# Loading and splitting the second third of queries and keys pair by pair in an attention kernel

## The chip, the cores and the metric

The kernel runs on one core of a Trainium2 chip. The metric is the device time of one execution in microseconds, as the median of three timed runs. The engines are TensorE (PE in the profile, with its weight load as PEld), VectorE (DVE), ScalarE (ACT), GpSimd (POOL) and SyncE (SP), which issues most transfers.

## The reference

```python
def _attn_ref(q, k, v):                       # 8 batches, 12 heads, 448 positions, 64 per head
    scores = scale * np.matmul(q, k.transpose(0, 1, 3, 2))
    scores = np.where(mask, -1000000000.0, scores)       # causal
    scores = scores - np.max(scores, axis=-1, keepdims=True)
    attn = np.exp(scores)
    attn = attn / (np.sum(attn, axis=-1, keepdims=True) + 1e-09)
    return np.matmul(attn, v).astype(np.float32)

def reference(**kwargs):
    attn_out = _attn_ref(**attn_kwargs)
    x = attn_out.transpose(0, 2, 1, 3).reshape(B * S, H * D)      # 3584 x 768
    return _moe_ref(x=x, **moe_kwargs)        # top-1 of 8 experts, 80 rows each, relu MLP 768-1024-768
```

All inputs are float32. The mixture of experts picks for each of 3584 rows the expert with the largest logit, keeps the 80 rows of an expert with the largest gate weights, and writes zero elsewhere.

## The kernel before

Attention comes first. Two heads form a pair, and 48 pairs (8 batches of 6) are worked one after the other. Queries and keys come from memory in *thirds*: a third is two pairs (a third of a batch's six), so third 0 holds pairs 0 and 1, third 1 holds pairs 2 and 3, third 2 holds pairs 4 and 5. `load_third` issues its transfers on SyncE: one for the queries and four for the keys, since the keys of each head are stored twice, once for each half of the partitions (`kf[0]`, `kf[1]`). Third 0 alone is loaded pair by pair. The buffers are two, so that third 2 takes the place of third 0.

Scores are wanted nearly in float32 but multiplied in float16. So each number is split: a high half (a cast to float16) and a low half (the number less its high half). `split_third` makes them: `q_high` and `k_high` cast, `q_low` and `k_low` subtract. For thirds 1 to 3 the casts are on DVE (half of third 1's queries on ACT), from third 4 on the query casts are POOL's; the subtractions are POOL's, except some of third 0, which are DVE's. A tile of scores is one product with the high half of the keys and one with the low half (L423 and L424 in the profile; the last rows of both heads share a tile, L433 to L436).

Each pair is worked in eight slots. Slots 0 to 6 give seven tiles of scores, slot 7 the product of probabilities and values of two pairs before (`xp`, L495). Behind a tile DVE masks it and takes the row minimum (L445, into `ns` and `nb`), and ACT takes the exponential into `prob` (L448). In slots 0, 2, 4 and 6 TensorE transposes the pair before's probabilities (L465), which ACT or DVE copies out (L477). The tiles of scores go round three banks, so a tile's products wait until the masking of the tile three before it is done. DVE copies a finished pair out (`xu`, L500).

The order on each engine is the order in which the program is written. What is not part of the eight slots is put in by a table: `later_on(slot, ...)` puts an operation at the end of a slot, counted from the start (pair n begins at slot 8n), and `third_plan` places the parts of a split by lists of such slots, `SECOND` for third 1 (counted from slot 0), `THIRD_EARLY` for thirds 2 and 3, counted from one slot after the third before begins. `late_constants` puts small constants of the routing at slots 19, 27, 35 and 43, on POOL: `identb` and `before`, `wgd`, `slots_e` with `slots_t` and `mv`, and the last memsets.

Each engine works through its own order and stops at an instruction whose inputs or buffers are not ready. After the last pair the mixture of experts follows, with weights loaded in pieces, products with weights split in the same way, and indirect transfers of the rows.

Of the kernel before, what the change touches and what calls it, by code (L numbers as in the profile page):

```python
# [35 lines left out]
THIRD = [0, 0, 2, 2, 4, 6, 8]  # L36
THIRD_NEXT = [0, 0, 6, 2, 6, 4, 8]
THIRD_EARLY = [0, 2, 4, 6, 4, 6, 8, 10]
SECOND = [8, 10, 6, 6, 10, 8, 12, 14]
ORDER_FIRST = [(0, 0), (1, 0), (2, 0), (0, 1), (1, 1), (2, 1)]  # L40
LATE = 19

# [10 lines left out]
def attention_then_moe(  # L53
# [12 lines left out]
    nc = tc.nc  # L66
# [71 lines left out]
    HB = 3  # L138
    PH = NP // HB
# [169 lines left out]
    lo, hi = slice(0, DH), slice(DH, P)  # L309

    def load_third(h):

        b, hf = h // HB, h % HB
        at = [0]

        def t32(n):
            at[0] += 1
            return qk_bufs[h % 2][:, (at[0] - 1) * PH * S:at[0] * PH * S].rearrange("k (p s) -> k p s", s=S)
        st = state[h] = {}
        st["qf"], st["kf"] = qf, kf = t32("qf"), [t32("kfa"), t32("kfb")]  # L320
        p0 = hf * PH
        for x in [slice(i, i + 1) for i in range(PH)] if h == 0 else [slice(0, PH)]:
            ps = slice(p0 + x.start, p0 + x.stop)

            begin = h == 0 and x.start == 0
            nc.sync.dma_start(qf[:, x], qT[b, :, ps, :])
            for j, rows in enumerate((lo, hi)):
                (nc.scalar if begin else nc.sync).dma_start(kf[j][lo, x], kT[b, rows, ps, :])
                nc.sync.dma_start(kf[j][hi, x], kT[b, rows, ps, :])
# [10 lines left out]
    def split_third(h):  # L340
# [3 lines left out]
        qf, kf = st["qf"], st["kf"]  # L344
        for x, nm in enumerate(("qa", "qb", "ka", "kb", "la", "lb")):
            st[nm] = qk_parts[h % 2][:, x * PH * S:(x + 1) * PH * S].rearrange("k (p s) -> k p s", s=S)
        qa, qb, k_hi, k_lo = st["qa"], st["qb"], (st["ka"], st["kb"]), (st["la"], st["lb"])

        sub = lambda e, o, a, b: e.tensor_tensor(out=o, in0=a, in1=b, op=ALU.subtract)  # L349
        v, g = nc.vector, nc.gpsimd  # L350
# [28 lines left out]
        def by_turns(x):  # L379
            def q_high(js=(0, 1)):  # L380

                for j in js:
                    copy = nc.gpsimd.tensor_copy if h > HB else nc.scalar.copy if h == 1 and j else nc.vector.tensor_copy
                    copy((qa, qb)[j][(lo, hi)[j], x], qf[(lo, hi)[j], x])  # L384

            def k_high(j):
                nc.vector.tensor_copy(k_hi[j][:, x], kf[j][:, x])  # L387

            def q_low(i):
                nc.gpsimd.tensor_tensor(out=qa[hi, i], in0=qf[lo, i], in1=qa[lo, i], op=ALU.subtract)  # L390
                nc.gpsimd.tensor_tensor(out=qb[lo, i], in0=qf[hi, i], in1=qb[hi, i], op=ALU.subtract)  # L391

            def k_low(i):
                for j in range(2):
                    nc.gpsimd.tensor_tensor(out=k_lo[j][:, i], in0=kf[j][:, i], in1=k_hi[j][:, i], op=ALU.subtract)  # L395
            lows = [f for i in range(x.start, x.stop) for f in (lambda i=i: q_low(i), lambda i=i: k_low(i))]
            highs = [q_high, lambda: k_high(0), lambda: k_high(1)]
            if h < HB + 1:
                return highs[1:] + [lambda: q_high([0]), lambda: q_high([1])] + [lows[1], lows[0]] + [f for i in range(1, PH) for f in (lows[2 * i + 1], lows[2 * i])]
            return highs + lows  # L400
# [575 lines left out]
        assert not steps  # L976

    def third_plan(h, slot):
        for x, f in zip(SECOND if h == 1 else THIRD_EARLY if h < HB + 1 else THIRD_NEXT if h % HB == 1 else THIRD, split_third(h)):
            later_on(slot + x, [f])  # L980

    with tc.manual_schedule():
# [26 lines left out]
        for i, pr in enumerate(pairs):  # L1009
# [8 lines left out]
            h = i // PH  # L1018
# [404 lines left out]
```

## Time and profile before

| | us |
|---|---|
| median of three timed runs | 470.98 |
| lowest and highest of them | 470.6 and 471.75 |
| the profiled execution | 472.62 |
| its span, first to last instruction | 470.9 |
| busy in the span: PE | 439.9 (93%) |
| DVE | 416.8 (89%) |
| ACT | 397.5 (84%) |
| POOL | 315.2 (67%) |
| mean granted TensorE clock | 0.985 of full |

Busy time is a mean over stages with different limits: POOL's 67% is made of a first half near 9 tenths and a tail with little work. The profiled execution's time is longer than its span by 1.72 us, which lie around the instructions.

### The profile page before, as it was taken

To read this page: it belongs to the slowest core of one execution; us is meant where nothing else is said; L and a number is where in the kernel's file an instruction comes from. 1 tells how busy PE (TensorE), PEld (TensorE's weight loads), DVE (VectorE), ACT (ScalarE), POOL (GpSimd) and SP (SyncE) were. 2 spreads that over 40 slices of the span, in tenths; PEclk is the share of its full clock that TensorE was granted. 3 is DMA by queue.
4 is the path that set the end of the run, shared out by engine and by line. 5 is a ranking of instruction groups with operands and counts; after the bars stand their busy time and mean duration, and the time that the engine had idled before them with its cause. 6 is when DMAs were issued, how large, how long until landed. Compare 5 with 4: busy or idle time off the path is not lost.

```text
span 470.9 us, 14816 instructions
## 1 busy us (share of the span) xinstructions
PE 439.9 (93%) x5279; PEld 344.2 (73%) x5279; DVE 416.8 (89%) x1279; ACT 397.5 (84%) x1076; POOL 315.2 (67%) x382
## 2 busy tenths in 40 slices
PE   4799999999999999999999999999989899898994
PEld 2566667866777777777777677676559899898994
DVE  5788889988998999899899989988589999998892
ACT  6798989878988897898889889887596999987992
POOL 7899999988987997897899699740361265400101
PEclk9799999999999999999999999999999999998998
DMA  7858899989769579776956967549939999999911
GB/s 215 185 151 235 266 291 246 274 251 314 197 200 295 170 217 290 219 222 203 289 178 209 308 172 229 171 168 378 386 112 333 410 388 390 387 423 427 386 38 43
DMA packets 43001, 120.88 MB, mean 257 GB/s; under 512 B 6146, under 2 KB 23810, under 8 KB 39472
## 3 DMA queue, kind: packets, MB, share of 16 engines
q1 hardware_dynamic: 41712, 116.21, 76.1%
q0 software_dynamic: 1056, 3.51, 2.4%
q8 instruction: 41, 0.67, 0.6%
q10 hardware_dynamic: 160, 0.23, 0.2%
q14 instruction: 32, 0.26, 0.2%
HBM read 96.36 MB, written 23.99 MB: 256 GB/s over the span
## 4 chain that ended last, share of the span: by engine, by line
PE 83%; DVE 7%; DMA 4%; issue 3%; SPq 1%; ACT 1%; POOLq 0%; DVEq 0%; POOL 0%; ACTq 0%
PE xp L495 17%; PE tp L465 16%; PE sp L423 7%; PE sp L424 5%; PE rt L592 4%; PE hp L1231 3%; DMA qk<-k_t 3%; PE sp L433 3%; PE gp L545 3%; PE hp L1241 3%; PE hp L1238 3%; PE hp L1240 3%; PE op L1241 3%; PE op L1238 3%; PE op L1240 3%
## 5 line engine op out<-in xcount | busy, mean ns | idle before, releaser
L448 ACT ACTIVATE prob<-ns,nb 128x128 f32<-128x128 f32 (+3 forms) x336 | 176.9, 528 | 23.7 <-DVE nb L445 21.7
L445 DVE CUSTOM_DVE_ANT_0 ns<-sp,mask 128x384 f32<-128x384 f32 (+2 forms) x288 | 116.1, 414 | 18.7 <-PE sp L424 14.8
L465 PE MATMUL tp<-ident,prob 128*128 128x128 f32 x768 | 118.0, 276 | 0.9 <-ACT prob L448 0.9
L477 ACT COPY PT<-tp 128x512 f32<-128x512 f32 x182 | 103.9, 572 | 17.6 <-PE sp L423 8.4
L395 POOL TENSOR_TENSOR qk<-qk,qk 128x448 f16<-128x448 f32 x92 | 96.4, 1069 | 14.2 <-DVE qk L387 8.6
L1165 DVE SCALAR_TENSOR_TENSOR wl<-wraw,wh 128x768 f16<-128x768 f32 (+1 forms) x98 | 98.1, 1062 | 4.0 <-ACT yt L1304 1.1
L465 PEld LDWEIGHTS tp<-ident,prob 128*128 128x128 f32 x768 | 89.7, 142 | 11.2 <-ACT PT L477 1.6
L495 PE MATMUL xp<-PT,vt 128*64 128x448 f32 (+3 forms) x768 | 91.1, 380 | 0.0
L1180 ACT ACTIVATE wh<-wraw 128x768 f16<-128x768 f32 (+1 forms) x98 | 84.7, 926 | 6.8 <-PE hp L1241 3.3
L495 PEld LDWEIGHTS xp<-PT,vt 128*64 128x64 f32 x768 | 53.8, 137 | 42.7 <-issue 22.7
L423 PE MATMUL sp<-qk 128*128 128x384 f16 (+2 forms) x288 | 75.7, 278 | 9.2 <-ACT qk L355 5.1
L424 PE MATMUL sp<-qk 128*128 128x384 f16 (+2 forms) x288 | 78.1, 277 | 1.2 <-DVE qk L349 0.4
L1241 PEld LDWEIGHTS <-wl 128*128 128x128 f16 x668 | 67.5, 101 | 3.2 <-issue 2.8
L1238 PEld LDWEIGHTS <-wh 128*128 128x128 f16 x668 | 67.9, 102 | 1.6 <-issue 1.6
L1240 PEld LDWEIGHTS <-wh 128*128 128x128 f16 x668 | 67.5, 101 | 1.1 <-issue 1.0
L1319 POOL DMA_INDIRECT out<-yo,idx x8 | 21.9, 2743 | 68.0 <-ACT yo L1316 64.8
L448 ACT ACTIVATION_READ_ACCUMULATOR prob<-ns,nb 128x1 f32 x336 | 63.7, 189 | 0.0
L390 POOL TENSOR_TENSOR qk<-qk,qk 64x448 f16<-64x448 f32 x46 | 53.7, 1168 | 4.0 <-DVE qk L384 0.6
L391 POOL TENSOR_TENSOR qk<-qk,qk 64x448 f16<-64x448 f32 x46 | 51.2, 1114 | 3.2
L387 DVE CAST qk<-qk 128x896 f16<-128x896 f32 x46 | 40.8, 888 | 0.9 <-DMA qk<-k_t 0.9
L384 POOL CAST qk<-qk 64x896 f16<-64x896 f32 x40 | 37.9, 948 | 4.3 <-PE sp L436 3.1
L423 PEld LDWEIGHTS <-qk 128*128 128x128 f16 x288 | 28.5, 99 | 16.8 <-issue 7.8
(188 smaller groups left out, 905.1 us busy)
## 6 DMA issues: line engine op xcount, KB each, us to landing
wraw<-w SPq DMA_DIRECT2D x27, 1536.0 KB, 22.0
qk<-k_t SPq DMA_DIRECT2D x92, 224.0 KB, 6.0
out<-mask_l SPq DMA_DIRECT2D x56, 192.0 KB, 4.5
qk<-q_t SPq DMA_DIRECT2D x23, 448.0 KB, 4.8
vt<-v_t SPq DMA_DIRECT2D x24, 384.0 KB, 5.9
xs<-xr SPq DMA_DIRECT2D x42, 192.0 KB, 3.8
wraw<-w SPq DMA_DIRECT2D x24, 256.0 KB, 4.8
vt<-v_t SPq DMA_DIRECT2D x24, 64.0 KB, 5.3
```

Source lines behind the costliest of these rows:

```text
L395: nc.gpsimd.tensor_tensor(out=k_lo[j][:, i], in0=kf[j][:, i], in1=k_hi[j][:, i], op=ALU.subtract)
L423: nc.tensor.matmul(sp[:, 0:w], qx[:, p, t * P:w], kx[:, p, 0:w], start=True, stop=False)
L424: nc.tensor.matmul(sp[:, 0:w], qx[:, p, t * P:w], lx[:, p, 0:w], start=False, stop=True)
L445: pr.masked = nc.vector.tensor_tensor_reduce(out=ns[:, 0:w], in0=sp[:, 0:w], in1=m, scale=-1.0 / 8.0, scalar=HUGE, op0=ALU.add, op1=ALU.mi ...
L448: nc.scalar.activation(pr.P[:, off:off + w], ns[:, 0:w], AF.Exp, bias=nb, scale=-1.0, accum_out=total)
L465: nc.tensor.transpose(pr.tp[:, i], pr.P[:, off:off + P], ident)
L477: copy(dst, src)
L495: state["pe"] = nc.tensor.matmul(xp[rows, 0:w], st["vt"][:, c, p * P + j * DH:p * P + (j + 1) * DH], pr.PT[:, j, n0:n0 + w], start=(c == 0 ...
L1165: return nc.vector.scalar_tensor_tensor(out=l, in0=src, scalar=SW, in1=h, op0=ALU.mult, op1=ALU.subtract)
L1238: nc.tensor.matmul(o, wh[:, ws], ah[:, c, :], start=(x == 0 and i % per == 0), stop=False, skip_group_check=True)
L1240: nc.tensor.matmul(o, wh[:, ws], al[:, c, :], start=False, stop=False, skip_group_check=True)
L1241: nc.tensor.matmul(o, wl[:, ws], ah[:, c, :], start=False, stop=(x == n - 1), skip_group_check=True)
```

## The change

Third 1 is loaded pair by pair, as third 0 was: ten transfers of half the size instead of five. Its split is made pair by pair too, in eleven steps at slots 8 to 15 instead of eight steps at slots 6 to 14: for its first pair (pair 2) the casts of queries (one half on DVE, one on ACT), two casts of keys on DVE, the query subtractions on POOL, and the two key subtractions on DVE instead of POOL; for its second pair (pair 3) the same, with all subtractions on POOL. Third 2, which was split in slots 17 to 27, is now split in slots 24 to 29 by a list of its own. All later thirds keep their slots.

```diff
--- before.py
+++ after.py
@@ -36,7 +36,8 @@
 THIRD = [0, 0, 2, 2, 4, 6, 8]
 THIRD_NEXT = [0, 0, 6, 2, 6, 4, 8]
 THIRD_EARLY = [0, 2, 4, 6, 4, 6, 8, 10]
-SECOND = [8, 10, 6, 6, 10, 8, 12, 14]
+SECOND = [8, 10, 11, 9, 11, 12, 13, 14, 15, 14, 15]
+THIRD_2 = [7, 8, 9, 10, 9, 10, 11, 12]
 ORDER_FIRST = [(0, 0), (1, 0), (2, 0), (0, 1), (1, 1), (2, 1)]
 LATE = 19
 
@@ -319,7 +320,7 @@
         st = state[h] = {}
         st["qf"], st["kf"] = qf, kf = t32("qf"), [t32("kfa"), t32("kfb")]
         p0 = hf * PH
-        for x in [slice(i, i + 1) for i in range(PH)] if h == 0 else [slice(0, PH)]:
+        for x in [slice(i, i + 1) for i in range(PH)] if h < 2 else [slice(0, PH)]:
             ps = slice(p0 + x.start, p0 + x.stop)
 
             begin = h == 0 and x.start == 0
@@ -393,6 +394,19 @@
             def k_low(i):
                 for j in range(2):
                     nc.gpsimd.tensor_tensor(out=k_lo[j][:, i], in0=kf[j][:, i], in1=k_hi[j][:, i], op=ALU.subtract)
+            def q_first(x):
+                v.tensor_copy(qa[lo, x], qf[lo, x])
+                nc.scalar.copy(qb[hi, x], qf[hi, x])
+
+            def k_first(j, x):
+                v.tensor_copy(k_hi[j][:, x], kf[j][:, x])
+
+            if h == 1:
+                a, b = slice(0, 1), slice(1, 2)
+                return [lambda: q_first(a), lambda: k_first(0, a), lambda: k_first(1, a), lambda: q_low(0),
+                        lambda: sub(v, k_lo[0][:, a], kf[0][:, a], k_hi[0][:, a]),
+                        lambda: sub(v, k_lo[1][:, a], kf[1][:, a], k_hi[1][:, a]),
+                        lambda: q_first(b), lambda: k_first(0, b), lambda: k_first(1, b), lambda: q_low(1), lambda: k_low(1)]
             lows = [f for i in range(x.start, x.stop) for f in (lambda i=i: q_low(i), lambda i=i: k_low(i))]
             highs = [q_high, lambda: k_high(0), lambda: k_high(1)]
             if h < HB + 1:
@@ -976,7 +990,7 @@
         assert not steps
 
     def third_plan(h, slot):
-        for x, f in zip(SECOND if h == 1 else THIRD_EARLY if h < HB + 1 else THIRD_NEXT if h % HB == 1 else THIRD, split_third(h)):
+        for x, f in zip(SECOND if h == 1 else THIRD_2 if h == 2 else THIRD_EARLY if h < HB + 1 else THIRD_NEXT if h % HB == 1 else THIRD, split_third(h)):
             later_on(slot + x, [f])
 
     with tc.manual_schedule():
```

What this does to the order of two engines. In the rows below `qk_112` and `qk_113` are the loaded queries and keys of even and odd thirds, `qk_0_114` and `qk_1_115` their halves, `ns,nb<-sp` a masking.

VectorE from the end of pair 0 through pair 1, before (casts of third 1 into `qk_1_115`):

```order
L384 CAST qk_1_115<-qk_113 64x896
L445 ISA ns,nb<-sp,mask_l 128x448
L445 ISA nb 128x1
L445 ISA ns,nb<-sp,mask 128x128
L445 ISA nb 128x1
L387 CAST qk_1_115<-qk_113 128x896
L445 ISA ns,nb<-sp,mask 128x128
L445 ISA nb 128x1
L445 ISA ns,nb<-sp,mask 128x256
L445 ISA nb 128x1
L387 CAST qk_1_115<-qk_113 128x896
L445 ISA ns,nb<-sp,mask 128x256
```

and after:

```order
L459 ISA ns,nb<-sp,mask 128x128
L459 ISA nb 128x1
L398 CAST qk_1_115<-qk_113 64x448
L459 ISA ns,nb<-sp,mask 128x128
L459 ISA nb 128x1
L459 ISA ns,nb<-sp,mask 128x256
L459 ISA nb 128x1
L402 CAST qk_1_115<-qk_113 128x448
L459 ISA ns,nb<-sp,mask 128x256
L459 ISA nb 128x1
L402 CAST qk_1_115<-qk_113 128x448
L350 TENSOR_TENSOR qk_1_115<-qk_113,qk_1_115 128x448
```

The whole-third cast ahead of pair 0's last masking and the whole-third key casts behind it are gone; casts of one pair stand two maskings later, and a subtraction follows them.

VectorE in the maskings before which third 2 (`qk_0_114`) is cast; before, in pair 2:

```order
L445 ISA ns,nb<-sp,mask 128x128
L445 ISA nb 128x1
L445 ISA ns,nb<-sp,mask 128x128
L445 ISA nb 128x1
L387 CAST qk_0_114<-qk_112 128x896
L445 ISA ns,nb<-sp,mask 128x256
L445 ISA nb 128x1
L445 ISA ns,nb<-sp,mask 128x256
L445 ISA nb 128x1
L387 CAST qk_0_114<-qk_112 128x896
L445 ISA ns,nb<-sp,mask 128x384
```

and after, in pair 3:

```order
L459 ISA ns,nb<-sp,mask 128x128
L459 ISA nb 128x1
L514 COPY xu<-xp 128x448
L388 CAST qk_0_114<-qk_112 128x896
L459 ISA ns,nb<-sp,mask 128x128
L459 ISA nb 128x1
L388 CAST qk_0_114<-qk_112 128x896
L459 ISA ns,nb<-sp,mask 128x256
L459 ISA nb 128x1
L385 CAST qk_0_114<-qk_112 64x896
L459 ISA ns,nb<-sp,mask 128x256
```

The four casts of third 2 have moved from pair 2 to pair 3, where they stand behind the copy of pair 0's output and have one masking, not two, between them.

GpSimd from the first constants on, before:

```order
L262 CAST identb<-ident 128x128
L265 MEMSET before 128x512
L267 AFFINE_SELECT before<-before 128x128
L395 TENSOR_TENSOR qk_0_114<-qk_112,qk_0_114 128x448 x2
L390 TENSOR_TENSOR qk_0_114<-qk_112,qk_0_114 64x448
L391 TENSOR_TENSOR qk_0_114<-qk_112,qk_0_114 64x448
L395 TENSOR_TENSOR qk_0_114<-qk_112,qk_0_114 128x448 x2
L273 MEMSET wgd 128x192
L276 COPY wgd<-lg 64x3x8 x4
L390 TENSOR_TENSOR qk_0_114<-qk_112,qk_0_114 64x448
L391 TENSOR_TENSOR qk_0_114<-qk_112,qk_0_114 64x448
```

and after:

```order
L263 CAST identb<-ident 128x128
L266 MEMSET before 128x512
L268 AFFINE_SELECT before<-before 128x128
L396 TENSOR_TENSOR qk_0_114<-qk_112,qk_0_114 128x448 x2
L274 MEMSET wgd 128x192
L277 COPY wgd<-lg 64x3x8 x4
L391 TENSOR_TENSOR qk_0_114<-qk_112,qk_0_114 64x448
L392 TENSOR_TENSOR qk_0_114<-qk_112,qk_0_114 64x448
L396 TENSOR_TENSOR qk_0_114<-qk_112,qk_0_114 128x448 x2
L391 TENSOR_TENSOR qk_0_114<-qk_112,qk_0_114 64x448
L392 TENSOR_TENSOR qk_0_114<-qk_112,qk_0_114 64x448
```

The constant `wgd`, which came behind three of third 2's four subtraction groups, now comes behind the first; nothing of third 2 stands ahead of the constants in either.

## Rows read from the trace of the kernel before

**Rows 1.** The head of the page: the span, and the span in 40 equal slices, each digit the busy share in tenths of TensorE (PE) and of GpSimd (POOL), and the granted TensorE clock in tenths of full speed.

```profile
span 470.9 us, 14816 instructions
...
PE   4799999999999999999999999999989899898994
...
POOL 7899999988987997897899699740361265400101
...
PEclk9799999999999999999999999999999999998998
```

**Rows 2.** The list of who waited for whom in the first 60 us: engine, its line, what it waited for, us in total, times, longest us.

```profile
PE sp L423 <- DVE nb L445: 3.9, 8, 1.0
```

**Rows 3.** The timeline of VectorE (DVE) from 9 to 33 us: start us, us, engine, line, operation, out<-in, shape, count, and in brackets the idle time before it and what ended it. L384 and L387 are the casts of queries and keys, L445 the masking of scores, L477 a copy of transposed probabilities.

```profile
11.51 0.62 DVE L384 CAST qk<-qk 64x896 f16<-64x896 f32 x1 [1.72 <-DMA qk<-q_t]
...
13.53 1.36 DVE L387 CAST qk<-qk 128x896 f16<-128x896 f32 x1 [0.65 <-DMA qk<-k_t]
...
15.73 0.81 DVE L387 CAST qk<-qk 128x896 f16<-128x896 f32 x1 [0.29 <-DMA qk<-k_t]
...
19.36 0.62 DVE L445 CUSTOM_DVE_ANT_0 ns<-sp,mask_l 128x448 f32<-128x448 f32 x1 [1.21 <-PE sp L436]
...
19.91 0.69 DVE L477 COPY PT<-tp 128x512 f32<-128x512 f32 x1
...
20.52 0.28 DVE L445 CUSTOM_DVE_ANT_0 ns<-sp,mask 128x128 f32<-128x128 f32 x1
...
20.99 1.36 DVE L387 CAST qk<-qk 128x896 f16<-128x896 f32 x1
...
22.96 0.61 DVE L387 CAST qk<-qk 128x896 f16<-128x896 f32 x1
...
26.64 0.29 DVE L445 CUSTOM_DVE_ANT_0 ns<-sp,mask 128x128 f32<-128x128 f32 x1
...
32.01 0.29 DVE L445 CUSTOM_DVE_ANT_0 ns<-sp,mask 128x128 f32<-128x128 f32 x1 [0.68 <-ACT prob L448]
```

**Rows 4.** The timeline of TensorE from 9 to 32 us, same columns. L423 and L424 are the first and second product of a tile of scores.

```profile
11.67 0.22 PE L424 MATMUL sp<-qk 128*128 128x128 f16 x1 [0.36 <-POOL qk L349]
...
21.15 0.27 PE L423 MATMUL sp<-qk 128*128 128x256 f16 x1
...
22.75 0.32 PE L423 MATMUL sp<-qk 128*128 128x384 f16 x1 [0.45 <-DVE nb L445]
...
25.83 0.23 PE L423 MATMUL sp<-qk 128*128 128x128 f16 x1
...
31.57 0.23 PE L423 MATMUL sp<-qk 128*128 128x128 f16 x1
```

**Rows 5.** The timeline of GpSimd (POOL) from 9 to 58 us, same columns; rows alike are merged and counted. L349, L390 and L391 subtract for the low halves of queries, L349 (once) and L395 for those of keys.

```profile
9.47 2.15 POOL L349 TENSOR_TENSOR qk<-qk,qk 64x448 f16<-64x448 f32 x2
...
20.84 1.03 POOL L391 TENSOR_TENSOR qk<-qk,qk 64x448 f16<-64x448 f32 x1
...
23.71 2.41 POOL L395 TENSOR_TENSOR qk<-qk,qk 128x448 f16<-128x448 f32 x2
...
33.20 1.31 POOL L391 TENSOR_TENSOR qk<-qk,qk 64x448 f16<-64x448 f32 x1
...
36.31 2.42 POOL L395 TENSOR_TENSOR qk<-qk,qk 128x448 f16<-128x448 f32 x2
...
50.64 1.31 POOL L391 TENSOR_TENSOR qk<-qk,qk 64x448 f16<-64x448 f32 x1
...
54.22 4.03 POOL L395 TENSOR_TENSOR qk<-qk,qk 128x448 f16<-128x448 f32 x4
```

**Rows 6.** Busy time of each engine in chosen stretches: the stretch, its length, us busy and instructions of PE, weight load, DVE, ACT, POOL, then the granted TensorE clock (1.00 is full speed), the DMA engines' busy share and GB/s moved.

```profile
4.00:6.00 2.00, 0.48 (x3) 0.42 (x4) 1.43 (x3) 1.13 (x2) 1.31 (x4) 1.00 0.83 269
...
14.00:16.00 2.00, 0.95 (x5) 0.58 (x4) 1.71 (x6) 1.20 (x5) 1.38 (x2) 0.50 1.07 271
...
9.80:13.20 3.40, 1.71 (x15) 1.20 (x14) 1.37 (x5) 2.39 (x6) 2.68 (x3) 1.00 1.03 239
...
13.30:20.00 6.70, 5.66 (x27) 3.63 (x25) 4.75 (x15) 4.78 (x17) 5.37 (x6) 0.50 1.03 242
...
23.70:56.30 32.60, 31.06 (x266) 22.06 (x268) 29.09 (x96) 30.17 (x99) 31.11 (x40) 1.00 0.74 204
```

**Rows 7.** The timeline of TensorE in pair 8, same columns as rows 4: the second product of pair 8's second tile of scores.

```profile
57.40 0.22 PE L424 MATMUL sp<-qk 128*128 128x128 f16 x1
```

**Rows 8.** The groups of instructions by line and shape over the first 60 us: line, engine, operation, out<-in, shapes, count | us busy, mean ns of one | idle time before them.

```profile
L445 DVE CUSTOM_DVE_ANT_0 ns<-sp,mask 128x384 f32<-128x384 f32 x16 | 8.7, 550 | 1.1 <-ACT prob L448 1.1
...
L445 DVE CUSTOM_DVE_ANT_0 ns<-sp,mask 128x256 f32<-128x256 f32 x17 | 6.6, 412 | 0.0
...
L445 DVE CUSTOM_DVE_ANT_0 ns<-sp,mask 128x128 f32<-128x128 f32 x18 | 5.1, 286 | 2.7 <-ACT prob L448 1.4 <-PE sp L424 1.3
...
L445 DVE CUSTOM_DVE_ANT_0 ns<-sp,mask_l 128x448 f32<-128x448 f32 x8 | 4.9, 617 | 2.0 <-PE sp L436 2.0
...
L349 DVE TENSOR_TENSOR qk<-qk,qk 128x448 f16<-128x448 f32 x3 | 1.9, 647 | 0.5 <-ACT qk L355 0.5
...
L356 DVE CAST qk<-qk 64x448 f16<-64x448 f32 x1 | 0.4, 385 | 2.2 <-DMA qk<-q_t 2.2
```

**Rows 9.** The timeline of SyncE's queue: an issue of a transfer, same columns as rows 3.

```profile
9.74 0.58 SPq L989 DMA_DIRECT2D lg<-wg  x1
```

## The prediction

> **What bounds the kernel now.** I read the head of the page first [rows 1]: TensorE (PE) is busy in 9 tenths of nearly every slice, GpSimd (POOL) nearly as much over the first half, and the granted TensorE clock is below full in the second slice. Next the list of who waited for whom in the first 60 us [rows 2]: TensorE's score products wait 3.9 us for VectorE (DVE) to free a score bank. Then DVE's timeline over pairs 0 to 4 [rows 3], which shows what DVE itself waits for: a transfer of queries, 1.72 us before the cast at 11.51, and of keys, 0.65 before the one at 13.53 and 0.29 before that at 15.73. They are what the change can remove. Last POOL's timeline [rows 5], the busy times by stretch [rows 6] and TensorE at pair 8 [rows 7], to see what a later split would meet: from 23.71 to 56.3 us POOL is busy 31.11 of 32.60 us, its gaps being some 0.08 us between instructions. It is a chain without slack inside. Its last link, the low halves of pair 8's keys, is two of the four subtractions that start at 54.22 and take 4.03 us together, so done at 56.24; pair 8's second products need them at 57.40. The reserve there is 57.40 - 56.24 - 0.06 (a hand-over, from POOL's end at 9.47 + 2.15 in [rows 5] to the product at 11.67 in [rows 4]) = 1.1 us.
>
> **The change part by part.**
>
> *Casts of the second third later and in pieces (pair 1).* Before, DVE runs from 9.72 to 20.52 (first masking of pair 2) with the 2.66 us of waits above and 1.21 us more at 19.36 for TensorE. After, the last masking of pair 0 and the first of pair 1 follow at once, and the first wait is at the second products of pair 1: these start at 11.67 in any case, held by POOL's subtractions [rows 4], so that masking starts at 11.95. From there to pair 2's first masking DVE has in its order: six maskings, 0.21 + 2 x 0.34 + 2 x 0.47 + 0.54 = 2.37 us (the means of [rows 8], less the 0.08 by which a successor starts earlier, as 19.91 after 19.36 + 0.62 in [rows 3]); five half-size casts at 0.39 - 0.06 = 0.33, 1.65 us; two subtractions of key lows that were POOL's, 2 x 0.60 = 1.20; one transpose copy, 19.91 to 20.52, 0.61. Sum 5.8 us, end 17.8. To this come waits for POOL. The casts at 13.53 and 20.99 took 1.36 us, that at 22.96 took 0.61: both long ones started while POOL was in a subtraction, and ended 0.48 after POOL's end (the one of 20.99 at 22.35, POOL's [rows 5] at 20.84 + 1.03); the short one met none. So a cast waits for POOL's current instruction, up to 1.03, and then takes the rest of its own time. POOL's query subtractions for pair 2 lie under two of the five casts (about 0.4 and 0.8 us), those for pair 3 perhaps under the last (0 to 0.85). Sum 1.2 to 2.05; I take 1.5: pair 2's first masking at N = 19.3 against 20.52, with ends 17.8 (no such wait) and 20.5 (all of them, and a late transfer). ScalarE's cast falls from one of 64x896 to two of 64x448 and hides behind this.
>
> *No split in pair 2.* Pair 2 loses its four casts on DVE, so TensorE paces it. From the products of its fourth tile, 21.15, to pair 3's first product, 25.83 [rows 4], there is one wait of 0.45 for DVE: 4.2 without. The fourth tile can start 0.35 after N, when the first masking (0.29) has freed its bank; pair 3's first products then start 4.2 later and take, with a hand-over, 0.25 to its first masking: T = 19.3 + 0.35 + 4.2 + 0.25 = 24.1, against 26.64: 2.5 us early. The ends of N give T = 22.6 and 25.3.
>
> *The whole split of third 2 in pair 3.* Here DVE has seven maskings (2.58), the output copy (0.54), the transpose copy (0.61) and four casts, at least 4 x 0.57: 6.0 us, against the 5.7 us that TensorE takes for pair 3 (25.83 to 31.57, [rows 4]). POOL starts on the first cast's result, so the next three casts meet it: 0.8, 0.7 and 0.2 us by the rule above. Pair 4's first masking is then at 24.1 + 7.5 = 31.6; it was 32.01 [rows 3]. Of 2.5 us, 0.4 is left.
>
> *POOL.* It loses two subtractions, 2 x 1.03, but in a stretch where it now waits for casts, so they bring nothing. It stands idle from about 23.7 and can start on third 2 only behind pair 3's first masking, copy and cast: 24.1 + 0.21 + 0.54 + 0.57 + 0.07 = 25.5, against 23.71: 1.8 us late. In third 2 it meets three casts instead of two (in [rows 5] a subtraction that met one took 1.31 instead of 1.03, two took 2.41 instead of 2.06): the third meeting is 0.28, and 0.17 goes where its second subtraction must wait for DVE's second cast, together 0.45. It is then 2.25 us late, and its chain runs on without gaps to pair 8, with about as many meetings as before (1.31 at 33.20, 2.42 at 36.31). The reserve of 1.1 is used up: pair 8's products come at 56.24 + 2.25 + 0.06 = 58.55 instead of 57.40, +1.15 us. Whatever pairs 4 to 7 have gained by then (0.4) is waited away. Behind pair 8 TensorE is again busy throughout (9 tenths), so the delay stays to the end.
>
> *Transfers.* Five more issues on SyncE's queue, up to 0.58 us each [rows 9], put the values, the gate weights and third 2's loads behind them later by up to 2.9 us. Third 2 was first cast at 20.99 without a wait for its transfer; now that comes at 24.9, 3.9 us later. Cost 0. If pieces landed late, a cast in pair 1 would wait: rival three.
>
> The Trainium skill ("SBUF — State Buffer", Who interferes with whom) has the casts' rule as an exclusive lock on a port pair shared by VectorE and GpSimd, the loser blocked for the whole instruction. The trace agrees for the cast (0.48 after POOL's end) but POOL loses 0.27 per meeting, not a cast's 0.6. With 0.6 the three meetings would add 1.0 instead of 0.45 and the sum would be +1.7; the row decides.
>
> Sum: +1.15 us on the profiled execution, 470.9 of span and 1.72 around it, 472.62 in all. That execution is 1.64 over the median of the three timed runs, 470.98; I put the same difference on the median: 472.1.
>
> **Rivals.**
>
> One, faster: the early gain is kept. For it: DVE's waits for transfers are real and up to 2.5 us of pair 3's start is gained. Against: POOL must then reach pair 8 sooner than now. That needs N near 17.8 (POOL only 0.3 late) and half of the 2.0 us that casts cost POOL from 23.71 to 56.3 (seven subtractions longer by some 0.28, the first and last in [rows 5] those at 23.71 and 50.64) avoided: 0.3 - 1.0 = 0.7 early, plus the reserve of 1.1, a gain of 1.8: 469.2.
>
> Two, slower: TensorE's clock. It stood at 0.50 of full (1.2 GHz) from 13.3 to 20.0, after a stretch in which TensorE was busy 1.71 of 3.40 us, and came back after 5.66 busy of 6.70 [rows 6]. Now TensorE has little to do between 13 and N, since DVE holds the banks; if the low clock comes later and lies over pair 2's second half, 1.7 to 3.4 of the 4.2 us there take as long again, and T and POOL's start come later by that: 472.1 + 1.7 = 473.8, up to 475.5. It decides from 0.3 us of such overlap, where 472.39 is passed. For it: DVE's 7 us of continuous work leaves TensorE waits; against: the low stretch may fall, as now, where DVE is the limit.
>
> Three, the change doesn't do what it says: the halved transfers are slower and casts still wait. Against: from 4 to 6 us, when pieces of the halved size were under way (the first third's), 269 GB/s were moved, from 14 to 16 us with pieces of twice the size 271 [rows 6]. A first piece late by 1 us puts N, T and POOL late by 1: 473.1. The Trainium skill ("DMA: Bandwidth & Descriptors", Bandwidth) advises batches of 1 MiB and calls transfers below 64 KB dominated by their descriptors; by it this rival gains weight, the rates above speak against it.
>
> Four, nothing: POOL is late by less than its reserve of 1.1, and what DVE gains and gives back leaves -0.4: 470.6.
>
> **How the numbers follow.** Forecast 0.45, its own range 471.3 to 473.0 (T by 0.9 either way); rival one 0.15; two 0.17; three 0.08; four 0.15. A measurement of this kernel tells 0.3%, 1.41 us, from no change: bounds 469.57 and 472.39. Slower: a third of the forecast (0.15), 0.16 of two, 0.06 of three, 0.37. Faster: rival one, 0.15. The same: 0.48. The range reaches from 469.3, most of rival one left out, to 474.2, the far half of rival two left out.
>
> **What would show it.** DVE's 1.72 us wait gone, and the first maskings of pairs 2, 3 and 4 near 19.3, 24.1 and 31.6. POOL idle for more than 1 us from about 23.7, its pair-8 subtractions ending near 58.5, and pair 8's products waiting for POOL. The granted clock tells rival two. I am wrong if pair 8's products don't wait for POOL, or if pair 4 starts more than 1.5 us earlier than now and pair 9 does too.

## The result, and the profile after

The changed kernel takes 474.92 us, the median of four timed runs (474.47 to 476.13), against 470.79 for the kernel before (median of four, 470.15 to 471.75): a ratio of 1.0076, 95% interval 1.0047 to 1.0106. It is 4.1 us slower. The forecast was 472.1 with a range up to 474.2.

The head of its profiled execution (474.92 us, span 473.0) answers to [rows 1]:

```profile
span 473.0 us, 14825 instructions
...
PE   4889899999999999999999999999989999999894
...
POOL 7669999988986997898798889750262265401101
...
PEclk9999999999999999999999999999999999999999
```

GpSimd has lost busy time in the second and third slices (12 to 35 us: 6 and 6, were 8 and 9), and the row of the granted TensorE clock has a 9 in all slices, where [rows 1] has a 7 in the second. But this row reads as full wherever the trace has no record of the clock, and the first record, of the full clock, starts at 17.05 us here and at 9.85 us in the kernel before. What the clock was until then shows in TensorE's own rows:

```profile
13.77 0.42 PE L437 MATMUL sp<-qk 128*128 128x256 f16 x1
13.98 0.42 PE L438 MATMUL sp<-qk 128*128 128x256 f16 x1
...
26.20 0.27 PE L437 MATMUL sp<-qk 128*128 128x256 f16 x1
26.31 0.27 PE L438 MATMUL sp<-qk 128*128 128x256 f16 x1
```

Products of this shape start 0.21 us apart at 13.77 and 0.11 apart at 26.20; in the kernel before they are 0.22 apart at 13.47, inside its stretch at 0.50 (1.2 GHz). So the changed kernel too runs its products at the lower level, up to 17.05.

The list of who waited for whom over the first 60 us, which answers to [rows 2], shows what GpSimd and TensorE now wait for:

```profile
DVE ns L459 <- PE sp L438: 4.2, 4, 1.4
POOL qk L396 <- DVE qk L388: 3.4, 1, 3.4
PE sp L437 <- DVE nb L459: 3.3, 7, 1.4
POOL qk L391 <- DVE qk L398: 3.3, 1, 3.3
```

GpSimd stands idle twice, 3.3 and 3.4 us, each time for a cast on VectorE; before, its longest wait of that kind was 0.64 us (ahead of its subtraction at 12.26). VectorE's timeline, to be read beside [rows 3] (L398 and L402 are the casts of one pair of third 1, L385 and L388 whole-third casts, L459 the maskings):

```profile
11.10 0.38 DVE L398 CAST qk<-qk 64x448 f16<-64x448 f32 x1
...
12.84 0.29 DVE L459 CUSTOM_DVE_ANT_0 ns<-sp,mask 128x128 f32<-128x128 f32 x1 [1.36 <-PE sp L438]
...
13.62 1.26 DVE L402 CAST qk<-qk 128x448 f16<-128x448 f32 x1
...
20.33 0.28 DVE L459 CUSTOM_DVE_ANT_0 ns<-sp,mask 128x128 f32<-128x128 f32 x1
...
25.30 0.29 DVE L459 CUSTOM_DVE_ANT_0 ns<-sp,mask 128x128 f32<-128x128 f32 x1 [1.28 <-PE sp L438]
...
27.68 1.12 DVE L385 CAST qk<-qk 64x896 f16<-64x896 f32 x1
...
32.86 0.29 DVE L459 CUSTOM_DVE_ANT_0 ns<-sp,mask 128x128 f32<-128x128 f32 x1 [0.27 <-PE sp L438]
...
46.35 2.78 DVE L388 CAST qk<-qk 128x896 f16<-128x896 f32 x1
```

VectorE's waits for transfers of third 1 are gone (its first cast starts at 11.10 with none). Pairs 2, 3 and 4 are first masked at 20.33, 25.30 and 32.86. In pair 6 a key cast of third 4 takes 2.78 us; the median of the 44 casts of this line is 0.62. GpSimd's timeline tells why, beside [rows 5] (L391 and L392 subtract for queries, L396 for keys, L257 sets constants to zero):

```profile
10.10 2.27 POOL L350 TENSOR_TENSOR qk<-qk,qk 64x448 f16<-64x448 f32 x2
...
17.93 1.12 POOL L391 TENSOR_TENSOR qk<-qk,qk 64x448 f16<-64x448 f32 x1 [3.30 <-DVE qk L398]
...
26.81 2.88 POOL L396 TENSOR_TENSOR qk<-qk,qk 128x448 f16<-128x448 f32 x2 [3.43 <-DVE qk L388]
...
31.34 1.03 POOL L391 TENSOR_TENSOR qk<-qk,qk 64x448 f16<-64x448 f32 x1
...
44.99 2.04 POOL L396 TENSOR_TENSOR qk<-qk,qk 128x448 f16<-128x448 f32 x2
46.96 0.27 POOL L257 MEMSET oh<- 128x200 bf16 x1
...
48.38 0.28 POOL L257 MEMSET row<- 128x80 bf16 x2
...
57.86 4.42 POOL L396 TENSOR_TENSOR qk<-qk,qk 128x448 f16<-128x448 f32 x4
```

Third 2 begins at 26.81 on GpSimd, not 23.71, and the four key subtractions that begin with pair 8's start at 57.86, not 54.22: 3.10 late has become 3.64. In pair 6, subtractions and memsets follow each other without a gap from 44.99 to 48.66, and the cast that began at 46.35, beside the second subtraction, ends at 49.13, 0.47 behind the last memset: it had waited for that subtraction and all six memsets. TensorE's timeline:

```profile
32.42 0.23 PE L437 MATMUL sp<-qk 128*128 128x128 f16 x1 [0.94 <-POOL qk L391]
...
33.54 0.23 PE L437 MATMUL sp<-qk 128*128 128x128 f16 x1 [0.38 <-POOL qk L392]
...
49.52 0.32 PE L437 MATMUL sp<-qk 128*128 128x384 f16 x1 [1.43 <-DVE nb L459]
...
59.95 0.22 PE L438 MATMUL sp<-qk 128*128 128x128 f16 x1
```

It waits for GpSimd in pair 4 (1.32 us), and in pair 6 for the maskings behind the long cast (1.43). Pair 8's second products, expected to be held by GpSimd, start at 59.95 (57.40 in [rows 7]) with no wait long enough to be listed: they come 0.16 behind the first ones, where 0.06 is usual, so they were held by some 0.1 us. The stretches of [rows 6] for the changed kernel, same columns:

```profile
13.30:20.00 6.70, 6.17 (x35) 4.14 (x34) 6.46 (x18) 5.88 (x17) 3.21 (x4) 1.00 0.92 258
23.70:56.30 32.60, 27.98 (x241) 20.54 (x238) 29.34 (x89) 27.22 (x87) 28.11 (x35) 1.00 0.56 147
```

From 13.3 to 20.0 the clock reads 1.00 (0.50 before), which by the products above holds from 17.05 on, and from 23.7 to 56.3 GpSimd is busy 28.11 us (31.11 before).

Where the loss sits is seen best from the start of each pair's last tile of scores (first product of that tile in TensorE's timeline). The table gives after and all experiments less the trace of before, whose own times stand in the first row, and in the last columns the start of GpSimd's pair-8 key subtractions and how long after it pair 9's last tile starts.

| us | pair 1 | 2 | 3 | 4 | 5 | 6 | 8 | 9 | 10 | 47 | GpSimd's pair-8 lows | to pair 9 |
|---|---|---|---|---|---|---|---|---|---|---|---|---|
| before, start | 18.23 | 23.60 | 29.34 | 34.87 | 41.96 | 48.01 | 62.02 | 67.83 | 74.78 | 325.33 | 54.22 | 13.61 |
| after | -1.01 | -0.96 | -0.15 | +1.46 | +0.77 | +2.36 | +2.55 | +2.47 | +2.75 | +3.10 | 57.86 | 12.44 |
| 1, third 2 back | -3.15 | +1.12 | +1.93 | +1.95 | +1.61 | +1.63 | +1.74 | +2.02 | +1.37 | +1.30 | 54.94 | 14.91 |
| 2, third 2 alone | -1.21 | -1.44 | -0.63 | +1.16 | +0.48 | +2.07 | +2.24 | +2.17 | +2.39 | +2.33 | 57.56 | 12.44 |
| 3, cast later | -0.90 | -0.46 | +0.35 | +2.15 | +1.46 | +1.47 | +3.26 | +3.17 | +3.44 | +3.71 | 58.59 | 12.41 |
| 4, constants later | -1.69 | -0.82 | -0.01 | +1.79 | +1.10 | +1.11 | +1.26 | +1.17 | +3.12 | +3.31 | 56.57 | 12.43 |
| 5, load alone | -0.09 | -0.56 | -0.57 | -0.57 | -1.55 | -0.77 | -0.60 | -0.67 | -0.39 | -0.36 | 54.73 | 12.43 |
| 6, constants in gap | -2.77 | +0.07 | +0.88 | +1.33 | +0.13 | +1.29 | +2.14 | +2.07 | +2.30 | +2.70 | 57.46 | 12.44 |
| 7, keys at 23 | -2.77 | -1.65 | -1.86 | -1.47 | -2.16 | -0.56 | -0.38 | -0.46 | -0.19 | -0.16 | 54.94 | 12.43 |
| 8, all at 23 | -1.00 | -0.92 | -0.29 | -0.29 | -0.99 | +0.60 | +0.79 | +0.71 | +0.98 | +1.36 | 56.10 | 12.44 |
| 9, as 7, memsets on VectorE | -3.05 | -1.44 | -1.65 | -1.27 | -1.95 | -1.95 | -1.79 | -1.86 | -1.63 | -1.66 | 53.52 | 12.45 |
| 10, before, memsets on VectorE | -0.94 | -1.01 | -1.01 | -1.01 | -1.04 | -1.03 | -1.04 | -1.33 | -1.26 | -0.96 | 52.79 | 13.71 |
| 11, after, memsets on VectorE | -3.29 | -1.67 | -0.86 | +0.93 | +0.25 | +0.26 | +0.42 | +0.35 | +0.62 | +0.61 | 55.73 | 12.45 |
| 12, whole third, keys at 23 | -0.48 | -0.92 | -1.14 | -0.76 | -1.44 | -1.44 | -1.30 | -1.38 | -1.15 | -1.22 | 54.02 | 12.43 |

Three things stand in it. The changed kernel is ahead by 1.0 us up to pair 2, behind by 1.5 at pair 4 and by 2.4 at pair 6. The lead is not shown to be the change's: run 10, whose order is that of before up to slot 39, has it too (0.94 and 1.01). The trace of before has the clock at 0.50 until 20.09, that of run 10 has the full clock from 16.85 on. And in eleven of the fourteen traces pair 9 follows GpSimd's subtractions by 12.41 to 12.45 us; in the trace of before it is 13.61. The difference, 1.17, is the reserve that GpSimd had there. Runs 5, 7, 9 and 12, which are as fast as before, are among the eleven: GpSimd can set the pace at pair 8 without being late.

### The profile page after: what moved, and what is told of

Same layout as the page of the kernel before. It is cut to its first block, busy times and chain, and to the rows that moved or that the text cites. A ratio compares the mean times of both kernels' runs of the same rounds, so it can differ in the third digit from the quotient of the medians.

```text
span 473.0 us, 14825 instructions
## 1 busy us (share of the span) xinstructions
PE 439.8 (93%) x5279; PEld 343.3 (73%) x5279; DVE 420.9 (89%) x1284; ACT 398.6 (84%) x1077; POOL 312.4 (66%) x380
## 4 chain that ended last, share of the span: by engine, by line
PE 78%; DVE 10%; issue 4%; ACT 3%; POOL 1%; DMA 1%; POOLq 0%; DVEq 0%; SPq 0%; ACTq 0%
PE xp L509 16%; PE tp L479 14%; PE sp L437 6%; PE sp L438 5%; PE rt L606 4%; PE hp L1245 3%; DVE ns L459 3%; PE gp L559 3%; PE sp L447 3%; PE hp L1252 3%; PE op L1255 3%; PE hp L1255 3%; PE hp L1254 3%; PE op L1252 3%; PE op L1254 3%
## 5 line engine op out<-in xcount | busy, mean ns | idle before, releaser
L459 DVE CUSTOM_DVE_ANT_0 ns<-sp,mask 128x384 f32<-128x384 f32 (+2 forms) x288 | 116.4, 414 | 21.9 <-PE sp L438 17.4
L396 POOL TENSOR_TENSOR qk<-qk,qk 128x448 f16<-128x448 f32 x90 | 95.2, 1079 | 16.5 <-DVE qk L388 10.8
L1252 PEld LDWEIGHTS <-wh 128*128 128x128 f16 x668 | 67.1, 100 | 1.6 <-issue 1.6
L1254 PEld LDWEIGHTS <-wh 128*128 128x128 f16 x668 | 66.7, 100 | 1.2 <-issue 1.2
L391 POOL TENSOR_TENSOR qk<-qk,qk 64x448 f16<-64x448 f32 x46 | 54.3, 1180 | 6.7 <-DVE qk L398 3.3
L392 POOL TENSOR_TENSOR qk<-qk,qk 64x448 f16<-64x448 f32 x46 | 50.5, 1097 | 3.3
L385 POOL CAST qk<-qk 64x896 f16<-64x896 f32 x40 | 37.5, 937 | 4.7 <-PE sp L450 3.5
L388 DVE CAST qk<-qk 128x896 f16<-128x896 f32 x44 | 39.5, 898 | 0.0
```

The costliest lines, as they stand in the source:

```text
L459: pr.masked = nc.vector.tensor_tensor_reduce(out=ns[:, 0:w], in0=sp[:, 0:w], in1=m, scale=-1.0 / 8.0, scalar=HUGE, op0=ALU.add, op1=ALU.mi ...
L1252: nc.tensor.matmul(o, wh[:, ws], ah[:, c, :], start=(x == 0 and i % per == 0), stop=False, skip_group_check=True)
L1254: nc.tensor.matmul(o, wh[:, ws], al[:, c, :], start=False, stop=False, skip_group_check=True)
```

## The experiments

Theory A: GpSimd's chain from third 2 to pair 8 starts 3.1 us later, because third 2 is cast later, and all pairs behind follow it. Theory B: the smaller transfers. Theory C: the waits at pairs 4 and 6 by themselves, not the chain behind them. Theory D (in run 5): the transfers cost nothing.

Each ratio is to the kernel before, timed beside that run. The intervals of runs 1, 2, 3, 6, 8 and 11 overlap that of the changed kernel (1.0047 to 1.0106), so how these differ from it rests on their traces; those of runs 5, 7, 9, 10 and 12 lie wholly below it, and that of run 4 wholly above. In the diffs, "..." stands for the rest of a line or for lines left out.

**1. The move of third 2 undone.**

```diff
-... SECOND if h == 1 else THIRD_2 if h == 2 else THIRD_EARLY if h < HB + 1 ...
+... SECOND if h == 1 else THIRD_EARLY if h < HB + 1 ...
```

> The changed kernel with third 2's split put back to slots 17 to 27; third 1 stays loaded and split pair by pair. Theory A (GpSimd begins third 2 at 26.8 instead of 23.7 us and is then late all the way to pair 8): GpSimd begins third 2 again near 23.5, pair 8's key lows end near 56.2, and the time is 470 to 471.3 us. Theory B (ten smaller transfers set the loss, through queries that land 0.5 us later and third 2's loads issued 2.2 us later): it stays at 473.5 to 475, or VectorE waits for transfers of third 2 near 21 us.

472.93 us (median of 12), ratio 1.0042 (1.0021 to 1.0063): between the two. GpSimd starts third 2 at 22.89 and pair 8's lows at 54.94, as A says, and the median is 2.0 us below the changed kernel's. But VectorE now waits for third 2's keys, issued from 14.04 on where before it was 12.42:

```profile
21.80 0.95 DVE L388 CAST qk<-qk 128x896 f16<-128x896 f32 x1 [1.71 <-DMA qk<-k_t]
```

The granted clock is at 0.50 (1.2 GHz) from 20 to 26 us, after a stretch in which TensorE was busy 4.57 of 6.70 us (columns as in [rows 6]):

```profile
13.30:20.00 6.70, 4.57 (x34) 2.97 (x33) 6.49 (x19) 5.77 (x18) 3.74 (x5) 1.00 0.92 234
20.00:26.00 6.00, 4.83 (x20) 2.98 (x21) 3.93 (x14) 3.89 (x13) 4.88 (x7) 0.50 1.03 228
```

Pair 1 is 3.15 us ahead and pair 2 1.12 behind. So in this run third 2's old slots did not suit the new load and split; what part the transfers and what part the clock had in it is not separated.

**2. The move of third 2 alone, in the kernel before.**

```diff
+THIRD_2 = [7, 8, 9, 10, 9, 10, 11, 12]
...
-... SECOND if h == 1 else THIRD_EARLY if h < HB + 1 ...
+... SECOND if h == 1 else THIRD_2 if h == 2 else THIRD_EARLY if h < HB + 1 ...
```

> The kernel before with third 2's split moved to slots 24 to 29 and nothing else. Theory A: GpSimd cannot begin third 2 before 26.5 us, its key lows of pair 8 end near 60, and the time is 474 to 475.5 us, the whole loss. Theory B: with the large transfers the loss is gone, 470.3 to 471.5 us.

474.26 us, 1.0072 (1.0053 to 1.0092). GpSimd begins third 2 at 26.33, pair 8's lows start at 57.56. One list of slots brings 3.2 us of loss without any change to the load or split of third 1. A holds, B falls as the main cause.

**3. The long cast of pair 6 moved, the chain left.**

```diff
-... THIRD_NEXT if h % HB == 1 else THIRD, split_third(h)):
+... [0, 4, 6, 2, 6, 4, 8] if h == 4 else THIRD_NEXT if h % HB == 1 else THIRD, split_third(h)):
```

> The changed kernel with third 4's first key cast four slots later on VectorE (slot 53 instead of 49), so that it no longer stands beside GpSimd's subtraction and memsets of constants, over which it took 2.78 us. Both theories on this place expect the 1.43 us wait of TensorE at 49.5 us to go. Theory A (GpSimd is 3.6 us late at pair 8 and its reserve there was 1.1): pair 8's products then wait 1.3 to 1.7 us for GpSimd's key lows, which still end near 59.9, and the time stays at 474.5 to 475.2. Theory C (the long cast alone costs the loss of pair 6): 473.2 to 473.7.

474.96 us, 1.0111 (1.0082 to 1.0139). The cast takes 0.73 us, TensorE's wait in pair 6 is gone, and the loss comes back at pair 8, where from pair 6 to 8 the lag grows from 1.47 to 3.26:

```profile
59.67 0.22 PE L438 MATMUL sp<-qk 128*128 128x128 f16 x1 [1.20 <-POOL qk L396]
```

This is the wait that the prediction named; in the changed kernel the long cast has taken its place.

**4. GpSimd's last constants behind pair 8.**

```diff
-            later_on(LATE + x * SLOTS, [f])
+            later_on(74 if x == 3 else LATE + x * SLOTS, [f])
```

> The changed kernel with GpSimd's last group of constants (six memsets, 1.77 us) at slot 74 instead of 43, behind pair 8's key lows and ahead of their first use. Theory A: the cast beside them is short again and GpSimd is 1.8 us earlier at pair 8, key lows ending near 58.1, so neither place costs anything; 1.6 to 2.2 us less, 472.7 to 473.4. If only the long cast mattered, the same 473.3, but then the run before this one would be as fast. If the chain behind pair 8 is what counts, no gain: 474.9.

477.25 us, 1.0143 (1.012 to 1.0166): slower than the changed kernel, against what I expected. The waits at pairs 6 and 8 went (lag 1.26 at pair 8, cast 1.16 us), but pair 10 pays for the moved work: TensorE waits for the first use of the constants,

```profile
73.65 0.40 PE L745 MATMUL selt<-identb,oh 128*128 128x128 bf16 x4 [0.96 <-POOL oh L716]
...
75.62 0.40 PE L745 MATMUL selt<-identb,mv 128*128 128x128 bf16 x4 [0.81 <-POOL mv L730]
```

1.77 us in all. GpSimd comes to L716 at 73.34, not earlier than in the changed kernel (73.01), and L730 itself takes 0.82 us (0.25 there). GpSimd has no slack there either. Its profiled execution took 475.34; the other timed runs took 2 us more, and what they lost has no trace.

**5. The load alone.**

```diff
-        for x in [slice(i, i + 1) for i in range(PH)] if h == 0 else [slice(0, PH)]:
+        for x in [slice(i, i + 1) for i in range(PH)] if h < 2 else [slice(0, PH)]:
```

> The kernel before with third 1 loaded in ten transfers instead of five and nothing else. The run with third 2 back in its old slots showed third 2's loads issued 2 us later and landing at 21.8 and 23.8 us, with VectorE waiting 1.71 us for them. Theory A: the same here, since third 2 is cast from 20.5 us on as before; VectorE waits 0.8 to 1.5 us in pair 2 and the time is 471.8 to 473. Theory D (the issues cost nothing, as the prediction put it): 470.3 to 471.5 us.

471.65 us, 1.0011 (0.9979 to 1.0042): between the ranges of A and D, and no cost that can be told, though the interval leaves room for 2.0 us. Third 2's loads are issued later here too, the first by 2.1 us (13.71, was 11.58), but VectorE does not wait for them: its first key cast of third 2 starts at 20.47 without a wait. The first cast of third 1 waits 2.58 us (1.72 before). Why third 2's keys landed later in run 1 is not shown.

**6. Constants in the idle stretch, the gate constant behind third 2.**

```diff
-            later_on(LATE + x * SLOTS, [f])
+            later_on((LATE, 35, 35, 22)[x], [f])
```

> The changed kernel with GpSimd's last six memsets (1.77 us) put into its idle stretch at 23.4 to 26.8 us, and the constant wgd (1.6 us) behind third 2's subtractions instead of between them. Theory A (a chain on GpSimd from 26.8 us to pair 8, that any work in front of it lengthens): the wait of TensorE for GpSimd at pair 4 (1.32 us) and the long cast of pair 6 go, but GpSimd is still some 1.8 us late at pair 8, where its reserve is 1.1: 1.4 to 2.0 us less than the changed kernel, 472.9 to 473.5. Theory C (the waits at pairs 4 and 6 are the loss, not the chain): 471.3 to 472.3.

473.98 us, 1.0049 (1.0025 to 1.0073), 0.5 us above A's range and far above C's. Pair 4 has no wait for GpSimd and the cast of pair 6 takes 0.90 us, yet the lag is there: GpSimd begins third 2 at 27.84 in this trace (the granted clock was 0.50 in pair 2, 20 to 23 us), and TensorE waits for it at pairs 6 and 8:

```profile
44.93 0.23 PE L437 MATMUL sp<-qk 128*128 128x128 f16 x1 [0.54 <-POOL qk L391]
...
58.55 0.22 PE L438 MATMUL sp<-qk 128*128 128x128 f16 x1 [0.26 <-POOL qk L396]
```

From its start to pair 8's lows GpSimd takes 29.62 us here and 31.05 in the changed kernel, so the work put into its idle time shortened the chain. C falls: pair 4's wait and the long cast are gone, but the median is only 0.9 us below the changed kernel's.

**7. Two casts one slot earlier.**

```diff
-THIRD_2 = [7, 8, 9, 10, 9, 10, 11, 12]
+THIRD_2 = [6, 6, 9, 10, 9, 10, 11, 12]
```

> The changed kernel with third 2's two key casts one slot earlier, at slot 23, into the 1.28 us in which VectorE waits for TensorE ahead of pair 3; nothing else. Theory A: GpSimd begins third 2 near 24.5 instead of 26.8 us, its key lows of pair 8 end near 57.7 instead of 59.9, and the time falls by 2 to 2.5 us to 472.3 to 473. If GpSimd's start doesn't set the loss, less than 0.7 us.

472.17 us, 1.0009 (0.998 to 1.0037): just below A's range, 2.75 us less than the changed kernel and the same as before. The casts fill VectorE's 1.28 us wait and GpSimd starts 2.8 us earlier:

```profile
24.01 2.30 POOL L396 TENSOR_TENSOR qk<-qk,qk 128x448 f16<-128x448 f32 x2 [1.31 <-DVE qk L388]
...
54.94 4.42 POOL L396 TENSOR_TENSOR qk<-qk,qk 128x448 f16<-128x448 f32 x4
```

The long cast of pair 6 is still there (2.79 us).

**8. All four casts there.**

```diff
-THIRD_2 = [7, 8, 9, 10, 9, 10, 11, 12]
+THIRD_2 = [6, 6, 6, 6, 8, 7, 9, 10]
```

> The changed kernel with all four casts of third 2 at slot 23, one after the other, and GpSimd's query subtractions for pair 4 ahead of its key subtractions. Theory A with its second part (a cast on VectorE waits until GpSimd's work without a gap is done, and costs GpSimd 0.28 us): GpSimd starts near 25.7 but meets no cast in pair 3, pair 3 loses none of VectorE's time to waiting casts (they took 1.12 and 1.20 us instead of 0.62), and the wait at pair 4 goes: 471.8 to 472.8 us. If only GpSimd's start counted and not the meetings: 473.6 to 474.

473.94 us, 1.0051 (1.0027 to 1.0074): not what A with its second part expected, but the time given for the start alone. The trace does not bear out that only the start counted. GpSimd started at 25.89, 0.92 earlier than in the changed kernel, and pair 8's lows at 56.10, 1.76 earlier, so its chain got 0.84 shorter as well. Pair 4's wait for GpSimd and the long casts of pair 3 went, but the long cast of pair 6 (2.78 us) stayed, and pair 8's lows are still 1.88 later than before, more than the reserve of 1.17. Nor does a cast wait for all of GpSimd's work without a gap, as the second part has it (see the last section).

**9 to 11. The six memsets on VectorE**, with run 7's slots, in the kernel before, and in the changed kernel.

```diff
-        def padded(shape, name):
+        def padded(shape, name, e=nc.vector):
...
-            nc.gpsimd.memset(t, 0.0)
+            e.memset(t, 0.0)
...
-            later_on(LATE + x * SLOTS, [f])
+            later_on((LATE, 27, 35, 39, 47)[x], [f])
```

> The changed kernel with third 2's key casts at slot 23, as in the run before, and the six memsets of the last constants (1.77 us on GpSimd) on VectorE, at slots 39 and 47. Theory A: third 4's key cast in pair 6 no longer takes 2.79 us, TensorE's wait of 1.44 us behind it goes, and GpSimd's key lows of pair 8 end near 55.3 us, ahead of the products: 1.0 to 1.9 us less than the run with the casts at slot 23 alone, 470.3 to 471.2. Rival: the memsets cost VectorE as much as they save, 471.8 to 472.6.

> The kernel before with the same six memsets on VectorE and nothing else. Theory A: GpSimd is not late there, its reserve at pair 8 only grows, so nothing is gained: 470.7 to 471.6 us, as the kernel before. If the memsets on GpSimd cost time in any order, 469.4 to 470.

> The changed kernel with the same six memsets on VectorE and nothing else. Theory A: the long cast of pair 6 goes, GpSimd's key lows of pair 8 end near 58.2 us, where the products then arrive at 58.3, and unlike the run that moved the memsets to slot 74 nothing has to be done later on GpSimd: 473.0 to 473.6 us against 474.9. If GpSimd's lateness at pair 8 didn't bind, 473.3 too, so this run tells from the memset run at slot 74 (477.2) that the work's place on GpSimd and not the cast made that one slow.

470.52 us for the first, 1.0005 (0.9989 to 1.0021); 470.95 for the control, 1.0012 (0.9984 to 1.0041); 472.93 for the changed kernel, 1.0052 (1.0024 to 1.0081). The first and second fall where A put them, the third 2.0 us below the changed kernel and just below its range. In run 9 the cast of pair 6 waits only for the subtraction beside it, the second of the two in GpSimd's row; VectorE's row and GpSimd's:

```profile
43.63 1.16 DVE L391 CAST qk<-qk 128x896 f16<-128x896 f32 x1
```

```profile
42.27 2.04 POOL L399 TENSOR_TENSOR qk<-qk,qk 128x448 f16<-128x448 f32 x2
```

In the kernel before, the same work taken off GpSimd is worth nothing, since GpSimd was not late. Nor is run 9 faster than before.

**12. Run 9 without the pair-by-pair load and split.**

```diff
-SECOND = [8, 10, 11, 9, 11, 12, 13, 14, 15, 14, 15]
+SECOND = [8, 10, 6, 6, 10, 8, 12, 14]
...
-        for x in [slice(i, i + 1) for i in range(PH)] if h < 2 else [slice(0, PH)]:
+        for x in [slice(i, i + 1) for i in range(PH)] if h == 0 else [slice(0, PH)]:
```

(and the split of third 1 in eight steps, as before)

> The run with third 2's key casts at slot 23 and the memsets on VectorE (470.52), but with third 1 loaded and split as in the kernel before, so it shows what the pair-by-pair load and split brings when GpSimd is not late. Theory A: GpSimd's start at third 2 and not the split of third 1 sets the time; 470.5 to 471.5. If the pair-by-pair split is itself worth the 1 to 2 us that pair 1 is earlier in the runs that have it: 471.8 to 472.8. If it costs time: 469 to 470.

470.3 us, 0.9984 (0.9962 to 1.0007), 0.2 below A's range and as run 9. Pair 1 is 2.6 us further ahead in run 9 (-3.05 against -0.48), of which 0.5 is left at pair 2 and 0.4 at the end. But even this is not shown to come from the split: the first record of the full clock starts at 11.46 in run 9 and at 18.91 in run 12. Where it starts near 17, pair 1 is ahead by 0.9 to 1.0 with third 1 split by pairs (after and runs 3 and 8) and by 0.94 with it whole (run 10). No version is faster than the kernel before by more than its interval.

## Why the prediction was wrong

**The mechanism was right, two sizes were not.** GpSimd stood idle (from 23.38 on, for 3.43 us; 23.7 was given), was late on third 2, ran on without gaps to pair 8 and had a reserve there of 1.1 (1.17 by the table). Run 2 shows that the later start alone makes most of the loss, run 7 that two casts one slot earlier undo it, run 3 that it binds at pair 8 when the cast of pair 6 does not hold TensorE before.

**The step that failed first is the start of third 2 on GpSimd.** In the terms below, N is the first masking of pair 2 and T that of pair 3. The prediction had "25.5, against 23.71: 1.8 us late"; it was 26.81, 3.10 late. The 0.45 for more meetings was nearly right (3.64 - 3.10 = 0.54). At pair 8 GpSimd was 3.64 late instead of 2.25; less the reserve of 1.17 that is 2.47, the lag of pair 9 (this must agree, since the 1.17 is taken from the same starts; the 1.1 of the prediction is the independent figure). Of the 1.3 us by which the start was missed, 1.0 came from N, at 20.33 instead of 19.3; from there the working held (4.97 us to T where 4.8 was put, 1.51 from T to GpSimd's start where it was 1.4). N was late because pair 1's second products were not held "in any case" until 11.67 but until 12.43: GpSimd's subtractions for pair 1 ended at 10.10 + 2.27, after 9.47 + 2.15 before, as the queries for its first cast landed later (cast at 7.09, was 6.53). The masking behind them came 0.9 late, at 12.84; from there to N it took 7.49 where 7.35 was put. In the fourteen traces those subtractions end between 11.62 and 12.70, and the trace of before, from which the 11.67 was taken, has the earliest. In run 11, with the same order there, the cast started at 6.83, pair 2 was first masked at 19.62 and GpSimd began at 26.10. So this part of the 1.3 differs from run to run; but 2.4 us of lateness is the least that a trace of this order shows, and 1.8 was put.

**The second is the last one, "the same difference on the median".** It is the larger of the two in the total. The 1.64 us by which before's profiled execution was above its median was for the larger part a stretch of that one execution: TensorE's clock was at 0.50 from 13.3 to 20.0 [rows 6]. In run 10, whose order on all engines is before's up to slot 39, the full clock is on record from 16.85 on, and all pairs from 2 to 8 start 1.0 us earlier. Against it the changed kernel loses 4.1 us by pair 47 (3.10 + 0.96), as much as the medians differ by. For ten of the thirteen kernels the column of pair 47 plus 0.96 gives the difference of its median from that of before within 0.4 us; runs 3, 4 and 6 are off by 0.8, 1.9 and 0.9. The rest of the 1.64 is in the tail behind pair 47: 145.57 us in before, with low digits of the clock in its last slices, 144.57 in after, and 142.89 to 146.53 over the fourteen traces.

**An early gain that was not there.** The prediction took 2.5 us as gained at pair 3, against the 26.64 of the trace of before. In run 10 pairs 2 and 3 are first masked at 19.18 and 25.62, so the changed kernel's 20.33 and 25.30 are 1.15 late and 0.3 early. The forecast did not hang on it, since the gain was to be waited away. Also, the terms listed for pair 3 add up to 7.7 us and not 7.5 (7.56 was measured, from 25.30 to 32.86); only the 0.4 us of gain that was left hangs on that.

**The account.** On the profiled execution 472.62 + 1.15 = 473.8 was predicted and 474.92 measured, 1.15 more: 1.39 for GpSimd, -0.07 for the reserve, 0.63 in pairs 10 and 19, -1.0 in the tail, 0.2 outside the span. The 0.63 and the -1.0 were no terms of the prediction; that they partly cancel is luck. With the 1.64 the 1.15 makes the 2.8 between 472.1 and 474.92.

**By its signs.** The 1.72 us wait went, as said. The three maskings came 1.0, 1.2 and 1.3 us later than given. Pair 8's subtractions started 3.64 late, so they ended about 1.4 later than the 58.5 given. "Pair 8's products wait for GpSimd" held by some 0.1 us only: pair 4's query subtractions and the cast of pair 6 had delayed TensorE by nearly as much already. I had looked only at the last link of the chain; GpSimd's lateness reached TensorE at two links before it.

**The rivals.** One (the early gain kept): no; but run 7 shows that it needed two casts one slot earlier. Two (the clock): not in the changed kernel, whose clock was full from 17.05 on, before pair 2's products; in runs 1 and 6 it stood at 0.50 over pair 2. Three (transfers): the changed kernel's casts wait for none, and run 5 shows no cost that can be told. Four (nothing): no. Nothing was said of a fifth that took part, a cast that waits through GpSimd's memsets (the prediction's rule, one instruction, held beside subtractions); its 1.6 us at pair 6 came out of the same lateness, so the loss would have come at pair 8 without it (run 3). The 0.35 us at pair 19 in after and in runs 3, 4, 6 and 8 was not looked into.

## What to carry to other kernels

When a split or load is moved, ask of the engine at its far end when it can start and what it does meanwhile; idle time on an engine whose later work has no slack is paid, less the reserve at the end, at whichever hand-over comes first. Work taken from the place where such a chain binds must leave the engine or go into its idle time (run 6), since put later it is paid later (run 4). Before an absolute time is carried from a profile to a median, look whether the profiled execution has a stretch at the low clock that the change may not have, and read it from the distance of the products too, not from the row of the clock alone.

## What the runs showed of the hardware

A cast on VectorE that starts while GpSimd subtracts ends 0.48 us behind that subtraction (0.25 when of half size), even where GpSimd's next subtraction follows without a gap: the cast at 27.68 in the changed kernel ends at 28.80, while the two subtractions beside it run from 26.81 to 29.69. The 1.16 us of runs 4, 9 and 11 is such a wait for one subtraction. It does not get in ahead of memsets: in pair 6 it ended 0.47 us behind one subtraction and six memsets (2.78 us; the same in runs 2, 7 and 8). What makes the difference is not shown. The Trainium skill ("SBUF — State Buffer", Who interferes with whom) has the loser of the shared port pair blocked for the whole instruction. The trace agrees beside subtractions; beside memsets the cast was held for seven instructions. GpSimd itself lost 0.26 to 0.28 us per meeting, 0.38 where the cast came in between two subtractions without a gap.

The largest of the memsets takes 0.95 us on GpSimd as 1024 elements and 0.48 on VectorE (run 9), which ran it as 512 elements of four bytes:

```profile
35.93 0.48 DVE L257 MEMSET ex<- 128x512 uint32 x1
```
